# Chunked attention feeding a routed mixture of experts: K block-diagonal over two heads, the zero fill moved, first up products moved, last routing batch reordered

## The chip, the cores and the metric

One core of a Trainium2 chip runs the whole program. The metric is device time in microseconds. The kernel before was run three times: 359.65, 360.88 and 364.33 us, median 360.88. One more execution was profiled; all rows of the trace in this document come from such profiled executions.

The engines that matter: PE (TensorE, matrix products and transposes; PEld is its weight load), DVE (VectorE), ACT (ScalarE), POOL (GpSimd, which here mostly issues DMAs) and SP (SyncE, which only issues DMAs). Every engine works through its own instructions in order and waits on semaphores for the others.

## The reference

Two stages. First, attention in chunks of 32 queries; each chunk sees 16 keys to the left, its own 32, 8 to the right (a window of 56) and 8 memory keys, so 64 scores per query:

```python
batch, n_heads, seq, head_dim = (4, 8, 768, 64)
for c in range(seq // 32):
    k_full = concat([mem_k, k[l_start:r_end]])
    a = softmax(scale * q_c @ k_full.T)
    out[c] = a @ v_full
```

The result, as 3072 tokens of 512 numbers, is `x` of the second stage, a mixture of 8 experts where each token goes to its best two:

```python
noisy_logits = x @ w_gate + log1p(exp(x @ w_noise)) * noise
top2 = the two largest of 8;  top2_w = softmax over them
for e in range(8): out[mask] += top2_w * (relu(x[mask] @ w1[e]) @ w2[e])   # 512 -> 1024 -> 512
```

## The kernel before

**Attention loop (lines 739 to 790).** A pair is two heads of one batch; there are 16 pairs (`NPAIR`), four per batch. The loop is pipelined over `i` = 0 to 16. In iteration `i` the engines get, in this order: the transposes of the softmax of pair i-1 (`PT_pe`, L296) and their copy (`PT_copy`, ACT, L301), maximum and subtraction for pair i (`max_dve`, L282 and L284), transposes and copy of Q of pair i+2 (`turn_pe`, L248 and L249), the value products of pair i-1 (`PV_pe`, L308 and L311), the exponential (`exp_act`, ACT, L289), gate logits of pair i-3 (`logits_pe`, L341), K of pair i+2 (`turn_pe`), the normalisation (`mult_dve`, L322 and L323), transposes of x for pair i-2 (`xT_pe`, L331, copy L333), and the scores of pair i+1 (`scores_pe`).

In `scores_pe` each head occupies 64 partitions, so each head has its own products: 12 with the memory keys (L261), 48 with the windows (L271), and 4 small ones that write -1e30 at the two ends of the sequence (L274): 64 matmuls per pair, each with a weight load. All other products and transposes of a pair are 72 matmuls.

**Loads.** q, k and v are loaded by POOL, six pairs ahead for q and k (`NQ`), and v into four buffers (`NV`). The weights of the first two experts follow in iterations 11 to 14 (`load_w1`, `load_w2`, 1 MB each as stored). The output must be zero before rows are added to it: SP writes 1 MB of zeros in each of iterations 9 to 14 (`zero_fill`, L568).

**Routing (`route`, L348 on).** After each batch of 768 tokens its logits become a list of small steps (s1 to s8): noise, rank of every expert (s1b, s2, s2b), gates (s2c, then s4, which also writes the batch's rows with `nc.sync.dma_start` to the scratch tensor `x_rows`), position of each token within its expert by triangular products (s3, s4b, s5), and a table of token numbers per expert and slot (s5b, s5c on POOL, s6, s7). The steps of batches 0 to 2 are spread over the following iterations (`steps`). `decode` turns a table into row indices, and `gather` has POOL read token rows from `x_rows` by index. Tables of the first batches already hold enough tokens for the first tiles of experts 0 and 1: `begin_first` (in iteration 13) gathers two tiles of 128 tokens for each with `idx_s`, and two further ones for each are gathered behind the loop with `idx_a`; the rest use `idx_f`, after the last batch.

**Experts (`every`, L681).** A generator that yields after each piece of work: `turn` transposes a gathered tile, `up` yields 8 units per half (each 4 matmuls into an `h` bank and a relu), `down` yields per tile of 128 tokens (8 matmuls of 512 columns, a scaling by the gate, and a scatter-add to `out` issued by POOL). `units(k)` runs k pieces. Behind the loop the last batch's routing steps are interleaved with 19 units by hand (L803 to L814); relus and tile copies there go to DVE or ACT by `cnt["by"]`. The order that follows: the four halves of `up` for experts 0 and 1 are 32 units, then `down` for both, then the others.

**Banks.** Transposes rotate through three PSUM banks (`tr`, ring `bankT`); `up` rotates through three (`hring`), which come into being when the loop's own banks are given back (`psE`).

Of the kernel before, what the change touches and what calls it, by code (L numbers as in the profile page):

```python
# [13 lines left out]
BF16 = mybir.dt.bfloat16  # L14
# [10 lines left out]
def kernel(  # L25
# [62 lines left out]
    def body():  # L88
# [107 lines left out]
        neg = const.tile([128, left_ctx], BF16, name="neg")  # L196
        nc.vector.memset(neg, NEG)
        mkT = ap_.tile([128, HP, B * n_mem], BF16, name="mkT", bufs=1)
# [37 lines left out]
        nc.scalar.copy(mkT, p_m)  # L236
# [5 lines left out]
        def turn_pe(n, x):  # L242
            nm, src = ("qT", "kT")[x], qks[n][x]
            dst = ap_.tile([128, 128, SJ], BF16, name=nm, bufs=3)
            p_t = bf16v(tr(), SJ, 128)
            for j in range(SJ):
                for hh in range(2):
                    nc.tensor.transpose(out=p_t[64 * hh:64 * hh + 64, j, :], in_=src[:, hh, j * D:(j + 1) * D], identity=identb)  # L248
            nc.scalar.copy(dst, p_t.rearrange("d j p -> d p j"))  # L249
            st[n][nm] = dst.rearrange("d p j -> d (p j)")  # L250
# [3 lines left out]
        def scores_pe(n):  # L254
            b, hp = divmod(n, HP)
            qT, kT = st[n]["qT"], st[n]["kT"]
            ps = bankS
            for u in range(BT):
                for hh in range(2):
                    hs = slice(64 * hh, 64 * hh + 64)  # L260
                    nc.tensor.matmul(out=ps[:, hh, u * CTX + WIN:(u + 1) * CTX], lhsT=qT[hs, 128 * u:128 * (u + 1)],  # L261
                                     rhs=mkT[hs, hp, b * n_mem:(b + 1) * n_mem], start=True, stop=True)
            for c in range(ncnk):
                u, r = divmod(c, 4)
                for hh in range(2):
                    hs = slice(64 * hh, 64 * hh + 64)
                    lo = left_ctx if c == 0 else 0
                    hi = WIN - right_ctx if c == ncnk - 1 else WIN
                    k0 = chunk * c - left_ctx
                    o = ps[32 * r:32 * r + 32, hh, u * CTX:u * CTX + WIN]  # L270
                    nc.tensor.matmul(out=o[:, lo:hi], lhsT=qT[hs, chunk * c:chunk * (c + 1)], rhs=kT[hs, k0 + lo:k0 + hi], start=True, stop=True)  # L271
                    for a, z in ((0, lo), (hi, WIN)):
                        if z > a:
                            nc.tensor.matmul(out=o[:, a:z], lhsT=onesb[hs, :chunk], rhs=neg[hs, :z - a], start=True, stop=True)  # L274
            st[n]["ps"] = ps[:, :, :BT * CTX].rearrange("p h (u c) -> p h u c", c=CTX)

        def bc4(ap, n):
            return ap.rearrange("p h (u o) -> p h u o", o=1).to_broadcast([128, 2, BT, n])

        def max_dve(n):  # L280
# [3 lines left out]
            nc.vector.tensor_tensor(out=sd, in0=st[n]["ps"], in1=bc4(mx, CTX), op=Alu.subtract)  # L284
            st[n]["sd"] = sd

        def exp_act(n):
            P = ap_.tile([128, BT, 2, CTX], BF16, name="P")
            nc.scalar.activation(out=P.rearrange("p u h c -> p h u c"), in_=st[n]["sd"], func=Act.Exp, scale=scale)  # L289
# [58 lines left out]
        def route(b):  # L348
# [38 lines left out]
            def s2c():  # L387
# [3 lines left out]
                gd = T("gd", [128, BT, E])  # L391
                nc.vector.tensor_tensor(out=gd, in0=nl, in1=bc(m1, E), op=Alu.subtract)
                R["ge"] = T("ge", [128, BT, E])
                nc.scalar.activation(out=R["ge"], in_=gd, func=Act.Exp)
# [13 lines left out]
            def s4():  # L408
# [5 lines left out]
                if b < B - 1:  # L414
                    nc.sync.dma_start(out=xd_part[b][b * S:(b + 1) * S].rearrange("(t p) r -> p t r", p=128), in_=xrows[b])
# [66 lines left out]

            if b == B - 3:
                return (s1,), (s1b, s2), (s2b, s2c), (s3, s4, s4b, spare_a), (s5, s5c, spare_b), (s5b, spare_c), (s6, s7, s8, spare_d, begin_first)
# [465 lines left out]
```

## Time and profile before

| what | value |
|---|---|
| three runs | 359.65, 360.88, 364.33 us |
| the profiled execution, time | 361.64 us |
| its span in the trace | 359.9 us |
| busy in the span: PE / PEld / DVE / ACT / POOL | 289.8 / 182.2 / 162.0 / 134.8 / 230.5 us |
| first maximum (L282) of pair 0 | at 12.67 us |
| last value products (L311) end the loop | at 121.2 us |
| the chain that ended last | the last scatter-add, L666, issued at 351.41 us |

How to read the rows. A row of the timeline gives the start in us, the duration, engine, line, operation, what it writes and reads, how many instructions were merged, and in brackets how long the engine had been idle before and what released it; "issue" means that the trace shows nothing that the engine was waiting for. A row of the waits view gives who waited for whom, the sum in us, how many times, and the longest. A row of the windows view gives a stretch, its length, then busy us and instruction counts for PE, PEld, DVE, ACT and POOL, the granted PE clock (1.00 is full), the mean share of the DMA engines, and GB/s.

### The profile page before, as it was taken

Reading aid. Unit: us, or ns where it says so; the run is one execution under the profiler, and the core shown is the slowest. Engines: PE = TensorE matmul, PEld = TensorE weight load, DVE = VectorE, ACT = ScalarE, POOL = GpSimd, SP = SyncE. Lnnn points to the kernel's source line nnn. Section 1 sums busy time; section 2 is a strip of 40 time slices with the busy share of each in tenths; the row PEclk is TensorE's granted clock in tenths of the full one; section 3 lists DMA queues with packets and bytes.
Section 4 is the critical chain, followed back from the end, with each engine's and each line's share of the span. In section 5 each row is a group of like instructions: output and inputs, shape, how many; then the busy total and the mean of one; then the engine's idle time right before and its main releaser. Section 6 shows DMA issues by size and latency. Waiting matters only on the chain. (4 is left out here: it accounts for less than half of the span.)

```text
span 359.9 us, 8635 instructions
## 1 busy us (share of the span) xinstructions
PE 289.8 (81%) x3583; PEld 182.2 (51%) x3597; DVE 162.0 (45%) x363; ACT 134.8 (37%) x273; POOL 230.5 (64%) x219
## 2 busy tenths in 40 slices
PE   0877788767756767799789999769999999999960
PEld 0755566655535556654555555425555555545420
DVE  7354538966858864432233343123333253323310
ACT  1656456665434326331333332303232432213210
POOL 8987737634533343567888878787887843748181
PEclk9997559985585578999999999969999999999995
DMA  9999999999999955249999999999999997959295
GB/s 106 159 162 185 169 134 122 259 310 150 282 300 233 230 109 124 62 67 169 248 166 194 171 239 164 247 173 190 217 177 189 199 124 115 131 70 131 38 121 74
DMA packets 99162, 60.36 MB, mean 168 GB/s; under 512 B 63536, under 2 KB 84016, under 8 KB 99120
## 3 DMA queue, kind: packets, MB, share of 16 engines
q0 software_dynamic: 82208, 49.84, 101.0%
q1 hardware_dynamic: 16624, 9.86, 9.7%
q8 instruction: 30, 0.49, 0.5%
q14 instruction: 12, 0.10, 0.1%
q10 hardware_dynamic: 288, 0.07, 0.1%
HBM read 65.07 MB, written 23.27 MB: 245 GB/s over the span
## 5 line engine op out<-in xcount | busy, mean ns | idle before, releaser
L638 PEld LDWEIGHTS <-w1t 128*128 128x128 bf16 x576 | 57.3, 101 | 54.5 <-issue 14.1
L666 POOL DMA_INDIRECT out_dram<-ys,idx_f x40 | 62.7, 1569 | 33.3 <-issue 16.0
L654 PE MATMUL bankE<-w2t,htf 128*128 128x512 bf16 x278 | 65.7, 379 | 0.5
L594 POOL DMA_INDIRECT xl<-x_rows,idx_f x48 | 50.0, 1041 | 21.7 <-issue 11.6
L638 PE MATMUL bankE<-xTf,w1t 128*128 128x416 bf16 x256 | 52.8, 349 | 5.7 <-DVE xTf L615 5.4
L665 DVE TENSOR_SCALAR ys<-bankE,gt 128x512 f32<-128x512 f32 (+1 forms) x32 | 21.9, 684 | 68.3 <-PE bankE L654 36.4
L133 POOL DMA_DIRECT2D vp<-in_v_dram x34 | 33.3, 986 | 21.7 <-PE bankO L311 10.8
L663 ACT ACTIVATE ys<-bankE,gt 128x512 f32<-128x512 f32 x24 | 16.5, 688 | 69.5 <-PE bankE L654 49.8
L654 PEld LDWEIGHTS <-htf 128*128 128x128 bf16 x288 | 27.3, 98 | 28.7
L623 DVE TENSOR_SCALAR htf<-bankE 128x416 bf16<-128x416 f32 x32 | 18.9, 591 | 27.5 <-PE bankE L638 25.9
L621 ACT ACTIVATE htf<-bankE 128x416 bf16<-128x416 f32 x32 | 16.6, 517 | 35.2 <-PE bankE L638 34.3
L638 PE MATMUL bankT<-xTf,w1t 128*128 128x416 bf16 x128 | 28.5, 346 | 0.3 <-DVE htf L623 0.3
L638 PE MATMUL bankE<-xTs,w1t 128*128 128x256 bf16 (+1 forms) x128 | 20.7, 302 | 3.9 <-ACT xTs L613 1.8
L282 DVE TENSOR_REDUCE mx<-bankS 128x12 f32<-128x768 f32 x16 | 15.3, 954 | 16.2 <-PE bankS L274 16.2
L654 PE MATMUL bankE<-w2t,hts 128*128 128x512 bf16 x92 | 21.5, 379 | 0.2
L611 PE MATMUL bankT<-identb,xl 128*128 128x128 bf16 (+1 forms) x224 | 19.8, 218 | 2.1 <-DVE xTf L615 1.5
L611 PEld LDWEIGHTS <-xl 128*128 128x128 bf16 (+1 forms) x224 | 15.4, 99 | 11.8 <-issue 4.4
L449 POOL TENSOR_TENSOR col<-mm_all,tl 128x672 f16<-128x672 f16 x4 | 8.0, 2012 | 18.6 <-DVE tl L436 18.6
L308 PE MATMUL bankO<-memv,PT 128*128 128x132 bf16 x96 | 12.0, 282 | 8.5 <-ACT PT L301 5.8
L301 ACT COPY PT<-bankT 128x768 bf16<-128x768 bf16 x16 | 12.8, 798 | 15.9 <-PE bankT L296 14.8
L249 ACT COPY kT<-bankT 128x768 bf16<-128x768 bf16 x16 | 12.7, 797 | 13.6 <-PE bankT L248 12.1
L284 DVE TENSOR_TENSOR sd<-bankS,mx 128x768 f32<-128x768 f32 x16 | 15.3, 958 | 1.4
(180 smaller groups left out, 469.1 us busy)
## 6 DMA issues: line engine op xcount, KB each, us to landing
w1t<-in_moe_w_dram POOLq DMA_DIRECT2D x8, 1024.0 KB
w2t<-in_moe_w_dram POOLq DMA_DIRECT2D x8, 1024.0 KB
out_dram<-zt SPq DMA_DIRECT2D x6, 1024.0 KB, 14.4
vp<-in_v_dram POOLq DMA_DIRECT2D x30, 168.0 KB
x_rows<-xrow SPq DMA_DIRECT2D x4, 792.0 KB, 8.7
qg<-in_q_dram POOLq DMA_DIRECT2D x16, 192.0 KB
kg<-in_k_dram POOLq DMA_DIRECT2D x16, 192.0 KB
xl<-x_rows,idx_f POOLq DMA_INDIRECT x48
```

The source lines that it names most:

```text
L133: nc.gpsimd.dma_start(out=vp[p0 + j:p0 + j + nj, c:c + m, hh, :], in_=bass.AP(v.tensor, v.offset + (hd * S + c * chunk + j - left_ctx) * D ...
L282: nc.vector.tensor_reduce(out=mx, in_=st[n]["ps"], axis=AX, op=Alu.max)
L284: nc.vector.tensor_tensor(out=sd, in0=st[n]["ps"], in1=bc4(mx, CTX), op=Alu.subtract)
L594: nc.gpsimd.indirect_dma_start(out=xl, out_offset=None, in_=xd, in_offset=bass.IndirectOffsetOnAxis(ap=idx[:, c:c + 1], axis=0), bounds_ch ...
L611: nc.tensor.transpose(out=p_t[:, kp, :w], in_=xl[:w, kp * 64:(kp + 1) * 64].bitcast(BF16), identity=identb[:w, :w])
L621: nc.scalar.activation(out=dst, in_=src, func=Act.Relu)
L623: nc.vector.tensor_scalar(out=dst, in0=src, scalar1=0.0, scalar2=None, op0=Alu.max)
L638: nc.tensor.matmul(out=h[:, :hi - lo], lhsT=W1[e][:, kp, f * 128:(f + 1) * 128], rhs=xTs[s][:, kp, lo:hi], start=(kp == 0), stop=(kp == KP ...
L654: nc.tensor.matmul(out=y, lhsT=ht[:, f, o:o + w], rhs=W2[e][:, f, :], start=(f == 0), stop=(f == FB - 1))
L663: nc.scalar.activation(out=ys[:, :wide], in_=y[:, :wide], func=Act.Copy, scale=gate)
L665: nc.vector.tensor_scalar(out=ys[:, :wide], in0=y[:, :wide], scalar1=gate, scalar2=None, op0=Alu.mult)
L666: ins = nc.gpsimd.indirect_dma_start(out=rows, out_offset=bass.IndirectOffsetOnAxis(ap=idx, axis=0), in_=ys[:, :wide], in_offset=None, bou ...
```

## The change

Five things change together.

1. **Scores.** K of a pair is stored block-diagonally, head 0 in partitions 0 to 63 of the first half, head 1 in partitions 64 to 127 of the second, zeros elsewhere, in two buffers zeroed once (`kbufs`); the memory keys likewise (`mkT`). One matmul over 128 partitions then gives both heads: 6 + 24 + 2 = 32 per pair in place of 64. The copy of K from PSUM becomes two copies, one per head, of 64 partitions each. The scores lie in another order, so that the exponential writes one run.
2. **Zero fill.** Issued behind the loop, in three writes of 2 MB, still by SP.
3. **Weights.** `load_w1(0)` in iteration 10, `load_w1(1)` in 12, `load_w2(0)` in 14, `load_w2(1)` behind the loop after the gathers with `idx_a`.
4. **First up products.** Eight units (the first half of expert 0) run in iterations 15 and 16, with `h` in the `tr` ring and relus on ACT. Expert 1's first two tiles are transposed between the last x transposes and the last logits.
5. **Last batch.** Ranks and positions (s2b, s3, s2c, s4b, s5, s5c) come in one group, then the gates' exponential (`s2d`), then s4 with s5b; the batch's rows are written by a DMA that ACT issues. 16 units are interleaved behind the loop in place of 19, so that 24 have been issued before `decode`, with the 8 of the loop.

```diff
-        mkT = ap_.tile([128, HP, B * n_mem], BF16, name="mkT", bufs=1)
+        mkT = ap_.tile([128, HP, B, 2, n_mem], BF16, name="mkT", bufs=1)
+        nc.vector.memset(mkT, 0.0)
+        kbufs = [ap_.tile([128, 2, S], BF16, name=f"kT{i}", bufs=1) for i in range(2)]
+        for kb in kbufs:
+            for hh in range(2):
+                nc.vector.memset(kb[64 * (1 - hh):64 * (1 - hh) + 64, hh, :], 0.0)
...
-            nc.scalar.copy(dst, p_t.rearrange("d j p -> d p j"))
+            if x == 0:
+                dst = ap_.tile([128, 128, SJ], BF16, name="qT", bufs=2)
+                nc.scalar.copy(dst, p_t)
+            else:
+                for hh in range(2):
+                    hs = slice(64 * hh, 64 * hh + 64)
+                    nc.scalar.copy(kbufs[n % 2][hs, hh].rearrange("d (p j) -> d p j", j=SJ), p_t[hs])
...
             for u in range(BT):
-                for hh in range(2):
-                    hs = slice(64 * hh, 64 * hh + 64)
-                    nc.tensor.matmul(out=ps[:, hh, u * CTX + WIN:(u + 1) * CTX], lhsT=qT[hs, 128 * u:128 * (u + 1)],
-                                     rhs=mkT[hs, hp, b * n_mem:(b + 1) * n_mem], start=True, stop=True)
+                nc.tensor.matmul(out=ps[:, u // UB, u % UB, :, WIN:], lhsT=qT[:, 128 * u:128 * (u + 1)], rhs=mkT[:, hp, b], start=True, stop=True)
             for c in range(ncnk):
-                for hh in range(2):
-                    nc.tensor.matmul(out=o[:, lo:hi], lhsT=qT[hs, chunk * c:chunk * (c + 1)], rhs=kT[hs, k0 + lo:k0 + hi], start=True, stop=True)
+                nc.tensor.matmul(out=o[:, :, lo:hi], lhsT=qT[:, chunk * c:chunk * (c + 1)], rhs=kT[:, :, k0 + lo:k0 + hi], start=True, stop=True)
...
-                if b < B - 1:
-                    nc.sync.dma_start(out=xd_part[b][b * S:(b + 1) * S].rearrange("(t p) r -> p t r", p=128), in_=xrows[b])
+                (nc.sync if b < B - 1 else nc.scalar).dma_start(out=xd_part[b][b * S:(b + 1) * S].rearrange("(t p) r -> p t r", p=128), in_=xrows[b])
...
+            if b == B - 1:
+                return (s1,), (s1b, s2), (s2b, s3, s2c, s4b, s5, s5c), (s2d,), (s4, s5b), (s6, s7)
...
-                    h = hring[cnt["h"] % 3]
+                    h = hring[cnt["h"] % 3] if hring else tr()
...
-            if NPAIR - 7 <= i < NPAIR - 1:
-                zero_fill(4 * (i - NPAIR + 7), 4)
-            if i == NPAIR - 5:
+            if i == NPAIR - 6:
                 load_w1(0)
             if i == NPAIR - 4:
-                load_w2(0)
-            if i == NPAIR - 3:
                 load_w1(1)
             if i == NPAIR - 2:
-                load_w2(1)
+                load_w2(0)
             steps(1 if i < NPAIR - 2 else 2)
+            if i >= NPAIR - 1:
+                units(FB // 2)
...
         for s in range(EARLY):
             gather(s, range(FIRST, SEALED), idx_a)
+        for x in range(3):
+            zero_fill(8 * x, 8)
+        load_w2(1)
         logits_pe(NPAIR - 2)
         xT_pe(NPAIR - 1)
-        units(2)
+        cnt["by"] = "dve"
+        for j in range(FIRST):
+            turn(1, j)
         logits_pe(NPAIR - 1)
-        begin, s12, s2, s34, s5, s5b, s678 = route(B - 1)
+        begin, *rest = route(B - 1)
         begin[0]()
         units(3)
         cnt["by"] = "act"
-        for g, more in ((s12, 2), (s2, 3), (s34, 2), (s5, 3), (s5b, 3), (s678, 1)):
+        for g, more in zip(rest, (3, 4, 1, 4, 1)):
             for fn in g:
                 fn()
-            if g is s34:
-                nc.sync.dma_start(out=last, in_=xrows[B - 1])
             units(more)
```

More of the change, by code (lines that the diff above doesn't have):

```diff
@@ L235, in body @@
             nc.tensor.transpose(out=p_m[:, hp, :], in_=mk_nat[:, 2 * hp:2 * hp + 2, :].rearrange("p h d -> p (h d)"), identity=ident)
-        nc.scalar.copy(mkT, p_m)
+        for hh in range(2):
+            nc.scalar.copy(mkT[64 * hh:64 * hh + 64, :, :, hh, :], p_m[64 * hh:64 * hh + 64].rearrange("p h (b m) -> p h b m", m=n_mem))
         st = [dict() for _ in range(NPAIR)]
@@ L263, in scores_pe @@
             for c in range(ncnk):
                 u, r = divmod(c, 4)
-                for hh in range(2):
[L266 to L274, printed above, removed]
@@ L280, in max_dve @@
+                for a, z in ((0, lo), (hi, WIN)):
+                    if z > a:
+                        nc.tensor.matmul(out=o[:, :, a:z], lhsT=onesb[:, :chunk], rhs=neg[:, :, :z - a], start=True, stop=True)
+            st[n]["ps"] = bankS[:, :, :UB * 2 * CTX].rearrange("p x (u c) -> p x u c", c=CTX)
         def max_dve(n):
@@ L685, in part @@
                 for j in range(lo // CAP, (lo + half) // CAP):
-                    turn(s, j)
+                    if s not in gts or (s, j) in got:
+                        turn(s, j)
                 yield from up(s, lo, lo + half)
```

42 lines of the change are left out of this document (23 added, 19 removed).

## The prediction, made before the changed kernel was run

> **What bounds the kernel now.** I read the page first, then the windows view over the stages, then PE's timeline through the attention loop, then the waits.
>
> ```profile
> PE 289.8 (81%) x3583; PEld 182.2 (51%) x3597; DVE 162.0 (45%) x363; ACT 134.8 (37%) x273; POOL 230.5 (64%) x219
> ```
>
> ```profile
> 24.34:107.23 82.89, 61.25 (x1664) 46.58 (x1658) 54.05 (x117) 46.89 (x66) 46.76 (x56) 0.73 1.60 210
> 107.23:121.45 14.22, 9.61 (x208) 7.41 (x206) 12.37 (x29) 6.13 (x10) 4.28 (x4) 0.50 1.30 227
> 121.45:146.65 25.20, 18.20 (x172) 14.53 (x170) 14.38 (x54) 10.24 (x28) 8.12 (x7) 0.76 0.58 128
> 180.00:348.00 168.00, 159.39 (x1019) 85.74 (x1029) 57.83 (x113) 51.68 (x129) 119.69 (x93) 0.98 0.98 161
> ```
>
> ```profile
> 24.34 0.95 DVE L282 TENSOR_REDUCE mx<-bankS 128x12 f32<-128x768 f32 x1
> ...
> 107.23 0.96 DVE L282 TENSOR_REDUCE mx<-bankS 128x12 f32<-128x768 f32 x1 [3.75 <-PE bankS L274]
> ```
>
> From 180 to 348 us PE is busy 159 of 168 us at nearly full clock: the experts are bound by PE, none of their work is taken away, and whatever is won ahead of them moves them earlier. What can be won lies ahead: from the maximum of pair 2 at 24.34 us to that of pair 14 at 107.23 (twelve pairs, 6.9 us each, PE at 0.73 of its clock and idle a quarter of the time), the last pairs, and 25 us behind the loop in which PE, granted 0.76, is idle 7 us while the last batch is routed.
>
> Why is PE idle in the loop? The waits view of 24 to 107 us puts this to "issue":
>
> ```profile
> PE bankS L271 <- issue: 3.7, 8, 0.7
> PE bankT L248 <- issue: 3.0, 2, 1.8
> PE bankO L308 <- ACT PT L301: 2.9, 9, 0.5
> PE bankO L308 <- issue: 2.6, 2, 2.2
> PE bankL L341 <- issue: 2.3, 1, 2.3
> PE bankS L261 <- issue: 2.2, 2, 1.3
> PE bankT L296 <- issue: 1.8, 1, 1.8
> ...
> ```
>
> The issue rows sum to 15.6 us, 1.3 per pair, and no other wait comes near. The timeline between two of these stalls:
>
> ```profile
> 38.59 0.53 PE L248 MATMUL bankT<-identb,qg 128*64 128x128 bf16 x6 [1.28 <-issue]
> 39.06 0.84 PE L308 MATMUL bankO<-memv,PT 128*128 128x132 bf16 x6
> 39.83 0.83 PE L311 MATMUL bankO<-vp,PT 128*32 128x128 bf16 x24
> 40.59 0.33 PE L341 MATMUL bankL<-wgn,xt 128*128 128x16 bf16 x6
> 40.85 0.85 PE L248 MATMUL bankT<-identb,kg 128*64 128x128 bf16 x12
> 41.63 0.82 PE L331 MATMUL bankT<-identb,xrow 128*128 128x128 bf16 x6
> 42.39 0.32 PE L261 MATMUL bankS<-mkT,qT 64*128 64x8 bf16 x12
> 42.64 0.26 PE L271 MATMUL bankS<-kT,qT 64*32 64x40 bf16 x8
> 42.69 0.18 PE L274 MATMUL bankS<-neg,onesb 64*32 64x16 bf16 x2
> 42.70 0.55 PE L271 MATMUL bankS<-kT,qT 64*32 64x56 bf16 x40
> 43.06 0.20 PE L274 MATMUL bankS<-neg,onesb 64*32 64x8 bf16 x2
> 43.19 0.60 PE L296 MATMUL bankT<-identb,P 128*128 128x128 bf16 x4
> 45.62 0.40 PE L296 MATMUL bankT<-identb,P 128*128 128x128 bf16 x2 [1.82 <-issue]
> ```
>
> ```profile
> q8 instruction: 30, 0.49, 0.5%
> ```
>
> From one stall to the next are 6+6+24+6+12+6+12+8+2+40+2+4 = 128 matmuls, each with its weight load: 256 instructions. The instruction queue moved 30 packets for 0.49 MB, about 16 KB each; PE's 3583 + 3597 instructions, in blocks of 256, are 28. So I read the stalls as PE waiting for its next block of instructions while data transfers fill the DMA engines (share 1.60). The block here lasted 45.62 - 38.59 = 7.0 us, of which 1.8 was the stall.
>
> [...]
>
> **Part 1, the scores.** A pair goes from 136 matmuls to 104. Twelve pairs are 384 fewer, three blocks of 128, and each remaining block covers 1.23 pairs instead of 0.94, so there is more work under each fetch. Without stalls an average pair takes 6.9 - 1.3 = 5.6 us; a block then holds 1.23 x 5.6 = 6.9 us of work against the 7.0 us block above. So most stall time should go: I take 12 of 15.6 us; the ends are 15.6 (all) and 15.6 x 32/136 = 3.7 (stalls as long as now, only fewer).
>
> PE time of the scores themselves: now 43.19 - 42.39 = 0.80 us. Afterwards, 24 products of 112 columns, priced by the 24 of 128 columns of L311 on the same 32-wide columns (40.59 - 39.83 = 0.76 us): 0.67; and 6 with the memory keys, by L341 (40.85 - 40.59): 0.26. That is 0.93, or +0.13 per pair, under 2 us for twelve. The gain is in the count, not in PE time.
>
> [...]
>
> ACT gets a second K copy per pair:
>
> ```profile
> 62.01 0.78 ACT L249 COPY kT<-bankT 128x768 bf16<-128x768 bf16 x1
> ```
>
> Half the partitions but the same 768 elements each, so I take the same 0.78 us for each; if the time went by partitions instead, two would cost what one does. ACT is busy 46.9 of 82.9 us in the twelve pairs; 9 us more do not make it the bound as a sum. On the path it delays the softmax transposes' copy, for which PE already waits 0.3 us in nine pairs: I put somewhat under half, 0.35 us a pair or 4 us in twelve, on the path; the ends are 0 and 9. Clock: the granted 0.73 should rise where the stalls go. I add -2 to the sum and make the rest a rival. With one answer: K's two buffers and Q's two instead of three are free in time, since the scores of pair i stand an iteration ahead of the copies for pair i+2; the exponential's new order has as many elements.
>
> Zeroing of the two K buffers and `mkT`:
>
> ```profile
> L165 DVE MEMSET vp<- 128x1536 uint32 x3 | 4.0, 1338 | 0.9 <-issue 0.9
> ...
> 19.37 0.85 PE L248 MATMUL bankT<-identb,qg 128*64 128x128 bf16 x12 [2.07 <-DMA qg<-in_q_dram]
> ```
>
> Four fills of a quarter of that element count are 1.3 us by proportion, 5.4 if each costs a full one. PE waits 2.07 us for q at 19.37 us, so I take nothing; the ends are 0 and 3. Sum for twelve pairs: -12 + 2 + 4 = -6 us, from -20 to +5. Taking 6 MB of zeros out of the loop frees DMA engines under the fetches that remain: I add -3 of the 3.6 us of stalls left over (0 to -3.6).
>
> **Parts 4 and 5, the last pairs and the last batch.**
>
> ```profile
> 129.29 0.21 ACT L356 ACTIVATE ns<-bankL 128x48 f32<-128x48 f32 x1 [3.27 <-PE bankL L341]
> 135.98 0.60 PE L638 MATMUL bankT<-xTs,w1t 128*128 128x256 bf16 x4 [3.23 <-ACT gt L616]
> 139.30 2.67 POOL L449 TENSOR_TENSOR col<-mm_all,tl 128x672 f16<-128x672 f16 x1 [3.94 <-DVE tl L436]
> ...
> 143.37 0.60 PE L638 MATMUL bankT<-xTs,w1t 128*128 128x256 bf16 x4
> ```
>
> Routing starts at 129.29 us, 8 us into the window that begins at 121.45, behind the last value products, because expert 0's transposes, copies and first two units stand between; then it takes 17.4 us to 146.65, where the gathers with `idx_f` begin. The position products (L399) stand in PE's order behind the units that start at 135.98, for which PE has waited 3.23 us, until expert 1's tile copies were done. The change removes both: expert 0's eight units go into pairs 15 and 16, and the position products no longer stand behind a tile copied on ACT. I take 3 us from the first 8, 3.2 for the wait, and 1 for the table step on POOL starting earlier relative to the gates: -7 (-3 to -11). Against it, eight units of at most 0.6 us and 8 transposes enter the last two pairs, where PE is busy 9.6 of 14.2 us: about 5 us of work in 4.6 us of holes, not all usable: +3 (0 to +5). Units ahead of `decode` rise from 19 to 24, so five leave the PE-bound stretch behind it: 5 x 0.6 = -3 (0 to -3).
>
> **Parts 2 and 3, zero fill and weights.**
>
> ```profile
> out_dram<-zt SPq DMA_DIRECT2D x6, 1024.0 KB, 14.4
> 118.07 0.37 SPq L415 DMA_DIRECT2D x_rows<-xrow  x1
> 156.80 1.64 POOL L666 DMA_INDIRECT out_dram<-ys,idx_a  x1 [2.49 <-DVE ys L665]
> SPq L813 <- DMA xl<-x_rows,idx_a: 1.3, 1, 1.3
> ```
>
> SP can start the zeros right behind its write of batch 2's rows (118.07 us now). Three megabytes at a time landed in about 14 us, so six need some 28: to 146 us, ahead of the first scatter-add at 156.80. That is the cover, some 10 us, and the rest shrinks it: the loop's gain moves both ends, the shorter routing only the scatter. If the zeros end late, POOL waits in order, and gathers and weight loads queue behind it. The last rows' write is now issued by ACT; on SP it waited 1.3 us for the `idx_a` gathers, which cost nothing there, but on ACT the relus behind it wait, and PE for them. The gathers and this write now share the engines with the zeros. SP's later read of the gates queues behind the zeros too; the expert stage that follows is 168 us long, so nothing waits for it. I take +2 (0 to +12).
>
> **Sum.** -6 -3 -7 +3 -3 +2 = -14 us, and -2 for the clock: -16. The profiled execution took 361.64 us for a span of 359.9, and the median of the runs is 0.8 below it: 360.9 - 16 = 345 us.
>
> **Rivals.**
> - *The stalls stay.* They are not instruction blocks, or last as long as the data transfers make them: then 3.7 us go instead of 12, the copies and products cost 6, and only the parts behind the loop pay: 345 + 8 + 2 = 355 us. For it: the waits view counts 16 stalls where 12 x 136 / 128 = 13 boundaries lie, and 8 of them stand before L271. Against: the count of 128 between two of the longest. Chance 0.12. [...]
> - *Scores slow down.* Both heads' products take turns where they ran together, 0.8 us a pair more, 13 us in 16, with half hidden under ACT: 345 + 6 = 351 us. Against: L311's 32 ns each. Chance 0.10. [...]
> - *The zeros starve the tail.* Slower. If the zeros share the DMA engines so that the `idx_a` gathers and ACT's row write land 15 us late, ACT holds the relus, PE stops, and the first scatter-add waits too; it decides once the zeros end after the gathers with `idx_f` are due. At half the measured rate six megabytes take 56 us, to 174: 17 past 156.80. With the loop's gain at its poor end (+5 in place of -9) and -7 behind it: 361 + 5 - 7 + 17 = 376; with a third of that delay 365. Against: the DMA share falls to 0.58 at 121 to 147 us. Chance 0.08.
> - *More clock.* Without stalls PE keeps full clock: the 61.3 us of PE work in the twelve pairs, granted 0.73, shrink by up to 0.27 x 61.3 = 17 us; with 10 of them on the path, 335 us. Chance 0.20.
>
> My forecast has 0.50. The forecast's own range is 338 to 352. **Range** 333 to 357: it takes in the clock case and the staying stalls. What a measurement of this kernel can tell from no change is about 2%, 7 us, so faster means under 353.7. Faster: 0.50 + 0.20 + 0.08 of the scores case = 0.78; same: 0.12 + 0.02 + 0.01 = 0.15; slower: 0.07.
>
> **What would show it.** The "issue" rows of PE in the loop fall from 15.6 to under 5 us, 128 matmuls apart where they remain, and a pair takes under 6.2 us. The scores take about 0.93 us at half clock. The K copies show twice per pair at 0.8 us. L356 of the last batch comes within 6 us of the last L311, and the first gather with `idx_f` within 14 us of L356. The zeros end before the first L666. It would be wrong if the issue rows stay, if ACT's row write stands idle for microseconds before it issues, or if the first L666 waits for the zeros.

## The result, and the profile after

| | before | after |
|---|---|---|
| median, range | 360.26 us, 359.23 to 364.33 (4 runs) | 349.19 us, 348.22 to 351.4 (4 runs) |
| profiled execution, span | 361.64, 359.9 us | 351.4, 349.3 us |

The ratio is 0.968, with a 95% interval from 0.959 to 0.977: faster, by 11 us where 16 were predicted. A second series on another chip gave 0.975 (0.971 to 0.979). Ratios here leave out runs over 1.5% above the fastest of their kernel, so they are not always the quotient of two medians, and the profiled executions of e3, e7, e10, e11 and e12 were of that slower kind.

The windows view of the changed kernel, over the twelve pairs from the maximum of pair 2 to that of pair 14 (stretch, its length, busy time of PE, PEld, DVE, ACT and POOL with their counts, granted PE clock, DMA share, GB/s):

```profile
24.72:94.25 69.53, 51.88 (x1280) 42.01 (x1281) 53.46 (x117) 55.37 (x77) 44.52 (x54) 0.85 1.80 176
```

They took 82.89 us before, so 13.4 went here, more than the 10.6 by which the whole span shrank. PE's waits in that stretch:

```profile
PE bankO L313 <- ACT PT L306: 5.5, 8, 1.0
PE bankT L483 <- DVE seen L477: 2.1, 1, 2.1
PE bankT L301 <- ACT kT L263: 2.1, 2, 1.4
PE bankO L316 <- issue: 1.2, 1, 1.2
...
PE bankT L336 <- issue: 1.0, 1, 1.0
...
```

Issue rows sum to 3.3 us now, from 15.6. At the top stand waits for ACT. ACT's timeline over one such pair (start, duration, what was read and written):

```profile
32.38 1.60 ACT L263 COPY kT<-bankT 64x768 bf16<-64x768 bf16 x2 [0.32 <-PE bankT L253]
34.00 0.80 ACT L338 COPY xt<-bankT 128x768 bf16<-128x768 bf16 x1
34.70 0.81 ACT L306 COPY PT<-bankT 128x768 bf16<-128x768 bf16 x1
35.39 0.82 ACT L257 COPY qT<-bankT 128x768 bf16<-128x768 bf16 x1
36.08 0.87 ACT L294 ACTIVATE P<-sd 128x768 bf16<-128x768 f32 x1
37.26 1.60 ACT L263 COPY kT<-bankT 64x768 bf16<-64x768 bf16 x2 [0.32 <-PE bankT L253]
```

From K copy to K copy are 4.88 us, and ACT stands idle for 0.32 of them: where neither a stall nor the routing's steps come in between, ACT is the fullest engine. Whether it sets the pair is tested in e4. The two K copies cost 0.8 us each: half the partitions took no less time than 128.

The loop's time also depends on the granted clock. PE's timeline at one of the stalls that remain, and the windows view around it in steps of 3.41 us:

```profile
43.33 0.61 PE L336 MATMUL bankT<-identb,xrow 128*128 128x128 bf16 x4 [1.00 <-issue]
```

```profile
35.86:39.27 3.41, 3.15 (x102) 2.68 (x99) 2.15 (x3) 3.05 (x5) 2.90 (x4) 1.00 2.40 153
39.27:42.68 3.41, 2.05 (x57) 1.39 (x51) 2.14 (x3) 3.09 (x5) 1.99 (x2) 1.00 2.06 166
42.68:46.10 3.42, 2.77 (x54) 2.44 (x54) 0.96 (x2) 2.33 (x4) 1.71 (x3) 0.50 1.87 169
46.10:49.51 3.41, 3.24 (x57) 2.45 (x54) 2.26 (x4) 2.69 (x6) 3.16 (x4) 0.50 2.19 167
49.51:52.92 3.41, 2.41 (x72) 1.94 (x73) 3.18 (x6) 3.37 (x5) 2.75 (x4) 1.00 2.21 163
```

The granted clock (third number from the end) falls from 1.00 to 0.50 at 42.68 us and comes back at 49.51. The stall ran from 42.33 to 43.33, so the fall came 0.35 us into it, and other idle times of 1.00 us (before 35.56 and 40.44 us) and 1.41 us (before 56.63) left the clock at 1.00: one stall does not decide it. PE was busy for 2.05 of the 3.41 us ahead of the fall. In the trace of this kernel, and in that of the one before, all changes of the clock lie whole multiples of 3.41 us apart. Cut into stretches of that length, the two traces show between 24 and 109 us: the clock fell after stretches in which PE was busy for 0.34 to 0.61 of the time and stayed full after 0.62 to 0.92; once halved, it stayed so after 0.39 to 0.90 and came back after 0.94 or more. From there to 130 us the same shares went with other outcomes: in this kernel the clock stayed full after 0.55 and 0.49 (stretches from 110.95, 121.19 and 124.60 us), and in the kernel before it came back after 0.83 (from 126.58 us). So the shares are readings of two loops, and no experiment set them alone. A stall counts in them with every other wait of PE in its stretch. In the kernel before, with three stalls between 32 and 46 us, the clock was 0.50 in all seven windows of 3 us from 33 to 54 us, the first and the last of which are:

```profile
33.00:36.00 3.00, 3.00 (x108) 2.40 (x100) 1.19 (x2) 1.41 (x2) 2.00 (x4) 0.50 1.80 177
...
51.00:54.00 3.00, 2.43 (x43) 1.84 (x29) 1.92 (x2) 1.58 (x3) 1.31 (x2) 0.50 1.88 128
```

Behind the loop, from the timelines of ACT and POOL:

```profile
118.45 0.21 ACT L361 ACTIVATE ns<-bankL 128x48 f32<-128x48 f32 x1 [0.61 <-PE bankT L620]
...
129.32 0.41 ACTq L421 DMA_DIRECT2D x_rows<-xrow  x1
```

```profile
137.55 1.13 POOL L603 DMA_INDIRECT xl<-x_rows,idx_f  x1 [10.78 <-DVE hts L632]
...
144.24 1.01 POOL L603 DMA_INDIRECT xl<-x_rows,idx_f  x1 [0.30 <-issue]
145.56 1.63 POOL L675 DMA_INDIRECT out_dram<-ys,idx_a  x1 [0.30 <-DVE xTs L624]
```

The last batch's routing starts at 118.45 us (129.29 before). Its rows are written from 129.32 on, and SP's read of the gates, which waits for this write, goes out at 136.96, 7.6 us later. Only then do the gathers with `idx_f` start, although their indices are ready at 133.72. (The releaser named in the gather's row had long been done; the write is what came last.) Then POOL issues six gathers and the first scatter-add without a gap: 8.0 us.

### The profile page after: what moved, and what is told of

It reads as the page before. It is cut to its first block, busy times and chain, and to the rows that moved or that the text cites. A ratio compares the mean times of both kernels' runs of the same rounds, so it can differ in the third digit from the quotient of the medians.

```text
span 349.3 us, 7639 instructions
## 1 busy us (share of the span) xinstructions
PE 277.5 (79%) x3071; PEld 175.5 (50%) x3085; DVE 161.4 (46%) x363; ACT 149.1 (43%) x295; POOL 228.9 (66%) x219
## 5 line engine op out<-in xcount | busy, mean ns | idle before, releaser
L647 PE MATMUL bankE<-xTf,w1t 128*128 128x416 bf16 x256 | 52.0, 346 | 5.4 <-DVE xTf L624 5.4
L263 ACT COPY kT<-bankT 64x768 bf16<-64x768 bf16 x32 | 25.3, 791 | 6.2 <-PE bankT L253 5.8
L647 PE MATMUL bankT<-xTs,w1t 128*128 128x256 bf16 (+1 forms) x88 | 15.2, 314 | 5.8 <-ACT hts L630 4.2
L647 PE MATMUL bankE<-xTs,w1t 128*128 128x256 bf16 (+1 forms) x104 | 16.0, 297 | 2.6 <-DVE xTs L624 1.3
L313 PE MATMUL bankO<-memv,PT 128*128 128x132 bf16 x96 | 9.9, 251 | 9.8 <-ACT PT L306 9.6
L455 POOL TENSOR_TENSOR col<-mm_all,tl 128x672 f16<-128x672 f16 x4 | 6.7, 1670 | 14.4 <-DVE tl L442 14.4
```

The source lines that it names most:

```text
L263: nc.scalar.copy(kbufs[n % 2][hs, hh].rearrange("d (p j) -> d p j", j=SJ), p_t[hs])
L647: nc.tensor.matmul(out=h[:, :hi - lo], lhsT=W1[e][:, kp, f * 128:(f + 1) * 128], rhs=xTs[s][:, kp, lo:hi], start=(kp == 0), stop=(kp == KP ...
```

## The experiments

Twelve kernels ran, on four chips; a time is given as the ratio to the kernel before on the same chip. The readings from which the verdicts come, one profiled execution each: the twelve pairs and what PE does in them (busy time, granted clock, issue rows, waits for ACT's copies PT, kT and xt),

| kernel | twelve pairs | PE busy | clock | issue | ACT copies |
|---|---|---|---|---|---|
| before | 82.9 | 61.3 | 0.73 | 15.6 | 4.0 |
| after | 69.5 | 51.9 | 0.85 | 3.3 | 9.6 |
| after, again (e9) | 69.1 | 50.9 | 0.88 | 1.7 | 9.5 |
| scores only (e1) | 74.1 | 51.2 | 0.85 | 3.5 | 9.3 |
| all but scores (e2) | 77.2 | 57.3 | 0.85 | 15.6 | 2.8 |
| 32 more matmuls (e3) | 80.6 | 61.7 | 0.73 | 10.6 | 5.8 |
| one K copy (e4) | 67.2 | 50.9 | 0.87 | 6.0 | 3.1 |
| zeros in the loop (e7) | 71.0 | 53.6 | 0.81 | 3.8 | 8.9 |

and the way from the loop to the end (us from the span's start; the write is that of the last batch's rows):

| kernel | last value product ends | routing starts | write issued | first `idx_f` gather | first scatter-add | end |
|---|---|---|---|---|---|---|
| before | 121.3 | 129.3 | 137.3 | 146.7 | 156.8 | 359.9 |
| after | 112.7 | 118.5 | 129.3 | 137.6 | 145.6 | 349.3 |
| after, again (e9) | 112.3 | 118.0 | 129.0 | 136.8 | 144.9 | 345.9 |
| e1 | 113.1 | 121.1 | 135.6 | 140.1 | 148.1 | 352.4 |
| w2 in the loop (e6) | 116.8 | 123.4 | 133.0 | 137.6 | 145.6 | 347.8 |
| e7 | 123.2 | 129.1 | 139.4 | 144.8 | 152.8 | 356.7 |
| units behind (e8) | 109.9 | 122.2 | 132.5 | 138.3 | 146.3 | 348.7 |
| w2 behind the loop (e10) | 112.9 | 118.7 | 136.9 | 141.6 | 149.5 | 351.8 |
| the same, relus on DVE (e11) | 114.9 | 120.6 | 134.6 | 139.6 | 147.5 | 351.9 |
| w2 behind a gather (e12) | 116.4 | 122.2 | 132.8 | 137.5 | 146.4 | 355.3 |

The expectations of e3 to e8 give 65.9 us for the twelve pairs of the changed kernel and 7.9 us for its waits on PT. Both were misread; 28.12 us, where the count of the pairs began, is the maximum of pair 3. Twelve pairs take 69.5 us, with 5.5 us of such waits.

**e1: the scores alone**, in the kernel before:

```diff
+        kbufs = [ap_.tile([128, 2, S], BF16, name=f"kT{i}", bufs=1) for i in range(2)]
...
-                    nc.tensor.matmul(out=o[:, lo:hi], lhsT=qT[hs, chunk * c:chunk * (c + 1)], rhs=kT[hs, k0 + lo:k0 + hi], start=True, stop=True)
+                nc.tensor.matmul(out=o[:, :, lo:hi], lhsT=qT[:, chunk * c:chunk * (c + 1)], rhs=kT[:, :, k0 + lo:k0 + hi], start=True, stop=True)
```

> The kernel before with the block-diagonal scores alone; zero fill, weights and the last batch's order stay as before. Theory A (PE waits for its next 256 instructions, so the number of PE instructions sets the loop): PE's issue rows between the maxima of pair 2 and pair 14 fall from 15.6 us to 4 to 6 although the zeros are still in the loop, these twelve pairs take 66 to 70 us instead of 82.9, and the run is 11 to 14 us faster than before, 347 to 350 us. Rival B (the stalls are made by the 6 MB of zeros that share the DMA engines with the fetches): the issue rows stay above 11 us, twelve pairs take over 77 us, the run is less than 5 us faster. Rival C (the gain of the whole change lies in the last batch): twelve pairs shorter by up to 17 us, but the end moves less than 5 us.

Ratio 0.985 (0.977 to 0.993). Theory A is right about the stalls: issue rows fall to 3.5 us though the zeros are still in the loop, so rival B is out. It is wrong about the time: the twelve pairs take 74.1 us, and the gain is some 5 us, not 11. What holds them, in PE's waits:

```profile
PE bankO L313 <- ACT PT L306: 5.6, 8, 1.0
PE bankO L316 <- DMA vp<-in_v_dram: 3.4, 2, 2.6
```

The values arrive late in a loop that runs faster while zeros and weights are moved beside it. What is due to the zeros and what to the weights is not separated here; e7, with the zeros alone put back, has no such wait in these pairs and 1.4 us of it behind them.

**e2: everything but the scores**, the changed kernel with the scores and the single K copy of before.

> The changed kernel with the scores and the single K copy of before; all other parts of the change stay. Theory A (number of PE instructions): issue rows of the twelve pairs at 12 to 16 us, twelve pairs take 78 to 83 us, the run is within 4 us of the kernel before (356 to 361 us). Rival B (zeros in the loop made the stalls): issue rows under 6 us, twelve pairs under 72 us, a run of about 350 us. Rival C (the last batch carries the gain): the loop as before, the run still 8 us or more faster.

Ratio 0.990 (0.984 to 0.995). The issue rows are at 15.6 us, exactly as before, with no zeros in the loop. So the prediction's -3 us, zeros making room for the fetches that remain, is refuted as a mechanism. Rival C is out too: some 4 us are won, not 8. The twelve pairs took 77.2 us, a little under theory A's 78, at a clock of 0.85 beside the same stalls; this execution had the highest mean clock of e2's ten (0.92, the others 0.86 to 0.91).

**e3: the number of matmuls restored**, with work that nobody reads:

```diff
+            for x in range(32):
+                r = x % 4
+                nc.tensor.matmul(out=bankS[32 * r:32 * r + 32, x // 16, 400:408], lhsT=onesb[:, :chunk], rhs=onesb[:, :8], start=True, stop=True)
```

> The changed kernel with 32 more matmuls per pair, of 8 columns each into columns of bankS that nobody reads, so that a pair has 136 matmuls again as before; output unchanged. By the 40 products of 56 columns that took 0.55 us before (14 ns each), 32 cost at most 0.45 us a pair. Theory A (number of PE instructions): the issue rows of the twelve pairs rise from some 4 to 10 to 16 us, twelve pairs take 74 to 83 us instead of 65.9, and the run is 8 to 16 us slower than the changed kernel. Rival D (the arithmetic or the shape of the new scores shortens the loop, not their number): issue rows stay under 6 us, twelve pairs lengthen by at most 5.4 us (12 x 0.45), the run by at most 6.

Ratio 1.000 (0.995 to 1.006): the whole gain is gone. The twelve pairs take 80.6 us, 11.0 more than in the changed kernel. Issue rows are back to 10.6. Between two of the longest stalls stands, in PE's timeline:

```profile
80.57 0.28 PE L272 MATMUL bankS<-mkT,qT 128*128 128x16 bf16 x5 [1.74 <-issue]
80.78 0.24 PE L279 MATMUL bankS<-kT,qT 128*32 128x80 bf16 x4
80.82 0.19 PE L282 MATMUL bankS<-neg,onesb 128*32 128x32 bf16 x1
80.85 0.41 PE L279 MATMUL bankS<-kT,qT 128*32 128x112 bf16 x20
81.10 0.17 PE L282 MATMUL bankS<-neg,onesb 128*32 128x16 bf16 x1
81.10 0.41 PE L285 MATMUL bankS<-onesb 128*32 128x8 bf16 x32
81.44 0.51 PE L304 MATMUL bankT<-identb,P 128*128 128x128 bf16 x6
81.87 0.53 PE L253 MATMUL bankT<-identb,qg 128*64 128x128 bf16 x12
82.84 0.52 PE L316 MATMUL bankO<-memv,PT 128*128 128x132 bf16 x6 [0.44 <-ACT PT L309]
83.28 0.52 PE L319 MATMUL bankO<-vp,PT 128*32 128x128 bf16 x24
83.74 0.31 PE L349 MATMUL bankL<-wgn,xt 128*128 128x16 bf16 x6
83.97 0.52 PE L253 MATMUL bankT<-identb,kg 128*64 128x128 bf16 x11
87.86 0.31 PE L253 MATMUL bankT<-identb,kg 128*64 128x128 bf16 x1 [3.36 <-issue]
```

The sum is 5+4+1+20+1+32+6+12+6+24+6+11 = 128 matmuls, with their weight loads 256 instructions. The stall does not fall on a step of the algorithm: it cuts the twelve K transposes after the eleventh. The fillers themselves took 0.41 us here, by estimate some 5 us in twelve pairs; the other 6 of the 11.0 come with the stalls and a clock that is back at 0.73. Rival D allowed 5.4 us in all, and is out.

**e4: without the second K copy**, to price it:

```diff
-                for hh in range(2):
+                for hh in range(1):
```

> The changed kernel without the copy of head 1's K (its rows in the K buffers stay zero), so the scores of every second head with the sequence's own keys are left out of the computation and its output is not the reference's. It prices the second copy. Theory E (ACT sets the loop of the changed kernel): PE's wait for the softmax transposes' copy falls from 7.9 us to 2 to 4 in the twelve pairs, these take 57 to 61 us instead of 65.9 (0.4 to 0.7 us of the copy's 0.79 a pair come back), and the run is 6 to 11 us faster than the changed kernel. Rival F (the clock or the stalls that remain set the loop, and the copy is hidden): twelve pairs within 2 us of 65.9, the run within 2 us.

Ratio 0.969 (0.963 to 0.976), as the changed kernel. PE's waits for PT fall to 2.9 us as theory E said, but the twelve pairs shrink by 2.3 us only, to 67.2: issue rows return from 3.3 to 6.0, and 2.2 us go to late Q loads (0.7 in the changed kernel). So ACT's second copy does not set the pair: most of what its removal frees is waited for elsewhere. Counted from 69.5 us, rival F is nearer: the copy is mostly hidden.

**e5: the second K copy on DVE:**

```diff
-                    nc.scalar.copy(kbufs[n % 2][hs, hh]...
+                    (nc.vector.tensor_copy if hh else nc.scalar.copy)(kbufs[n % 2][hs, hh]...
```

> The changed kernel with head 1's K copy on DVE instead of ACT; nothing is left out. Theory E (ACT sets the loop): ACT loses 0.79 us a pair; DVE, busy 54 of 82.9 us before, takes one more copy a pair. The pair shortens by 0.2 to 0.6 us, PE's wait for the softmax transposes' copy falls below 5 us of 7.9, the run is 3 to 8 us faster than the changed kernel. Rival F (copy hidden, or DVE becomes the bound in ACT's place): twelve pairs within 2 us of 65.9 or longer, the run within 2 us of the changed kernel or slower.

Ratio 1.025 (1.019 to 1.031), slower than before the change; twelve pairs 87.0 us. The waits view of DVE shows why:

```profile
DVE kT L263 <- ACT kT L263: 16.9, 11, 2.0
```

The two halves are written one after the other, so DVE stands and waits for ACT's half, and everything queued behind the copy on DVE waits with it; then PE waits 12.6 us for that copy. The run does not say what two copies side by side would cost.

**e6 to e8: three moves behind and in the loop.** e6 issues expert 1's second weights in the last pair instead of behind the zeros:

```diff
+            if i == NPAIR - 1:
+                load_w2(1)
...
-        load_w2(1)
```

> The changed kernel with expert 1's second weights issued in the last pair of the loop instead of behind the zeros, so ahead of the gathers with idx_a. Theory G (ACT's write of the last batch's rows lands late, 7.6 us instead of 3.8 before, because it shares the DMA engines with that 12 us load): the write lands in 4 to 5 us, the gathers with idx_f start 2 to 4 us earlier than 137.55 us, and the run is 2 to 4 us faster. Rival H (the write shares with the zeros, or its form is slow on ACT's queue): it still lands 7 us or more after its issue, the run within 1.5 us. Against the edit: POOL's gathers with idx_a stand behind the load's issue, and instruction fetches in the last pairs share with it.

The write lands as theory G said:

```profile
133.02 0.41 ACTq L421 DMA_DIRECT2D x_rows<-xrow  x1
```

```profile
137.06 0.37 SPq L850 DMA_DIRECT2D gov<-x_rows  x1
```

That is 4.0 us, not 7.6, so ACT's queue is not slow (rival H). But the gathers start no earlier, since this execution's loop ended 4 us later: pair 13 took 10.7 us, where the changed kernel needed 7.0. The edit is not shown to be the reason, as the load is issued behind that pair, and e12, whose loop is that of the changed kernel, needed 9.9. Ratio 0.959 (0.951 to 0.967), some 3 us below the first series of the changed kernel and 6 below the second, though not beside either on one chip. It may be the best version of all; that is not settled.

e7 puts the zeros back into the loop, 1 MB in each of six passes:

```diff
+            if NPAIR - 7 <= i < NPAIR - 1:
+                zero_fill(4 * (i - NPAIR + 7), 4)
...
-        for x in range(3):
-            zero_fill(8 * x, 8)
```

> The changed kernel with the zero fill back in six iterations of the loop, 1 MB in each. Theory A with the prediction's term for it (3 us, 0 to 3.6): issue rows of the twelve pairs rise from some 4 to 5 to 8 us, the run is 1 to 4 us slower. Rival B (zeros in the loop made the stalls): issue rows over 10 us, the run 8 us or more slower. Rival J (zeros do nothing in the loop once it has fewer instructions, and behind the loop they delay the tail): the run is the same or up to 3 us faster.

Ratio 0.983 (0.976 to 0.989), some 5 us slower than the first series and 3 than the second, on other chips. The issue rows stay at 3.8 us, below theory A's 5 to 8 and far below rival B's 10, and the twelve pairs cost 1.5 more. The loss lies in the last pairs, where the last value product ends 10.5 us later than in the changed kernel. PE's timeline there:

```profile
115.76 1.04 PE L620 MATMUL bankT<-identb,xl 128*128 128x128 bf16 x8 [8.19 <-DMA xl<-x_rows,idx_s]
```

and POOL's, ahead of it:

```profile
97.47 0.81 POOL L556 DMA_DIRECT2D w1t<-in_moe_w_dram  x1 [6.52 <-DMA vp<-in_v_dram]
98.66 1.16 POOL L603 DMA_INDIRECT xl<-x_rows,idx_s  x1 [0.37 <-DVE rec L327]
103.55 1.04 POOL L603 DMA_INDIRECT xl<-x_rows,idx_s  x1 [3.73 <-DMA w1t<-in_moe_w_dram]
```

Expert 0's work in the last pairs needs rows that are gathered late, since POOL waits in order for late values and weights. So the two edits depend on each other: with the zeros in the loop, PE waits 8.2 us for the units' rows.

e8 leaves the zeros behind, and takes the units out of the last pairs:

```diff
-            if i >= NPAIR - 1:
-                units(FB // 2)
...
+        units(FB)
```

> The changed kernel with expert 0's eight first up products behind the loop, ahead of expert 1's transposes, instead of four in each of the last two passes. Theory K (they fill holes of PE in the last two pairs, but only in part): the last value product ends 3 to 5 us earlier than 112.7 us, routing of the last batch starts within 1.5 us of 118.4 us, and the run is 0 to 3 us slower. Rival L (in the loop they cost their full time, since ACT's relus stand in line with the copies that set the pair): the last value product is 5 us or more earlier, the routing starts 1.5 us or more earlier, the run is 1 to 3 us faster.

Ratio 0.970 (0.964 to 0.976), no difference that can be told. The last value product ends 2.8 us earlier (theory K: 3 to 5), routing starts 3.7 us later, and as the row write then lands in 5.2 us, the first scatter-add comes 0.7 us later. Theory K holds for the time of the run, not for the start of routing.

**e9 to e11: where to put the load**, beside the changed kernel itself. e9 is the changed kernel itself. e10:

```diff
+        load_w2(1)
         decode(tabs[(B - 2) % 2][:, :EARLY * NT], idx_a, None)
...
-        load_w2(1)
```

and e11 besides:

```diff
-        cnt = {"h": 0, "y": 0, "flip": 0, "by": "act"}
+        cnt = {"h": 0, "y": 0, "flip": 0, "by": "dve"}
```

> The changed kernel once more, as the measure for the two that run with it on this chip. By the ratio of its first runs, 0.968 of the kernel before; twelve pairs in 68 to 71 us, the last rows' write 7 to 9 us ahead of the first gather with idx_f, and some 203 us from the first scatter-add to the end, as in every kernel so far (201.5 to 204.3).

> The changed kernel with expert 1's second weights issued directly behind the loop, ahead of the decoding for idx_a, so some 12 us earlier (about 109 instead of 121.6 us) and not in the loop. Theory G (the last rows' write lands late because that load shares the DMA engines with it): the first gather with idx_f stands 4 to 5.5 us behind the write's issue instead of 8.2, the first scatter-add comes 3 to 4 us earlier, and as it is some 203 us from there to the end, the run is 3 to 4 us faster than the changed kernel beside it. Rival H (the write is slow on ACT's queue, or the zeros delay it): 7 us or more as now, the run within 1.5 us. Rival M (PE bounds everything behind decode, so an earlier scatter-add is not an earlier end): the write lands early, and the run is within 1 us.

> As the run before it, and the relus, tile copies and gates of expert 0's first up products in the last two pairs on DVE instead of ACT. Theory N (in the last two pairs ACT is the bound, so that work of expert 0 lengthens the pairs through ACT): the last value product ends 1 to 3 us earlier, the run is 1 to 3 us faster than the run before it. Rival O (DVE is as full there as ACT, or the units cost PE's own time): within 1 us, or slower by up to 2.

Ratios 0.975 (0.971 to 0.979), 0.976 (0.971 to 0.981) and 0.977 (0.972 to 0.982): no difference. In e10 the first gather stands 4.7 us behind the write's issue, so theory G holds once more. But in this execution the write is issued 8 us later than in e9, and PE's timeline shows why:

```profile
131.66 1.19 PE L620 MATMUL bankT<-identb,xl 128*128 128x128 bf16 x8 [7.04 <-DMA xl<-x_rows,idx_a]
```

With weights as well as zeros ahead of them, the gathers with `idx_a` landed in 13.7 us (6.7 in the changed kernel). PE waited for them, ACT for PE, and the write stands behind that work in ACT's order. The span of this execution is 5.9 us longer than e9's, while the ratios do not differ, so a delay of this size is shown for this execution alone. In e11 the last value product ends 2.0 us later than in e10, and PE waits for DVE instead (rival O).

**e12: the load behind the first gather:**

```diff
-            gather(s, sets[s][1], idx_f)
+            gather(s, sets[s][1][:1], idx_f)
+            if s == EARLY:
+                load_w2(1)
+            gather(s, sets[s][1][1:], idx_f)
```

> The changed kernel with expert 1's second weights issued behind the first gather with idx_f instead of ahead of the last batch, some 13 us later (about 135 instead of 121.6 us). Theory G (the last rows' write lands late because that load shares the DMA engines with it): with the zeros done by then, the write lands 3.8 to 5 us behind its issue instead of 7.6, the first gather with idx_f starts 3 us earlier. The load costs POOL 1.0 us among the gathers and lands 8 to 12 us later, at 143 to 147 us, about when the second expert's down products want it (148.7 less 3): the first scatter-add comes 1.5 to 2.5 us earlier, the run is 1 to 3 us faster than the changed kernel. Rival P (the load then shares with the gathers and PE waits for it): the write lands early all the same, the gathers land 6 us or more behind their issue instead of 2.9, the run is the same or up to 4 us slower. Rival H (the write is slow on ACT's queue whatever runs beside it): it lands 7 us or more behind its issue.

Ratio 0.982 (0.975 to 0.988): above both series of the changed kernel, though the intervals overlap and the chips differ. That fits rival P (the same or up to 4 us slower), and theory G's gain did not come. The write lands in 4.0 us, with the load out of the way:

```profile
132.84 0.41 ACTq L421 DMA_DIRECT2D x_rows<-xrow  x1
```

```profile
136.88 0.37 SPq L851 DMA_DIRECT2D gov<-x_rows  x1
```

and PE waits for the gathers that are now issued around it:

```profile
PE bankT L620 <- DMA xl<-x_rows,idx_f: 6.3, 1, 6.3
```

Theory G is shown for the write itself. In e6, e10, e11 and e12, where the load is elsewhere, the write lands in 4.0 to 4.1 us. Beside the load it takes 4.8 us in e7, 5.2 in e8, 7.2 in e9 and 7.6 in the changed kernel; in the last two the load, issued at 121.11 and 121.56 us, lands 12.9 and 13.0 us later, 5.0 and 5.2 us behind the write's issue. In the trace of the changed kernel 208 packets of the load begin between the first and the last of the write's 784. The zeros' last packet there had ended at 126.2 us, 3.2 us before the write was issued, so the zeros do not delay it. An earlier write is not yet an earlier end: in e10 and e12 something else then came late (rows for PE by 7.0 and 6.3 us), with the zeros, two weights, two sets of gathers and the write all issued between the loop's last pairs and the first scatter-add.

## Why the prediction was right, and where its sizes were off

The direction, the main mechanism and the range held; the forecast was 4 us too low. Term by term, from the two profiled executions (10.6 us of span; the terms are rounded):

| step | predicted | measured |
|---|---|---|
| up to pair 2, and twelve pairs (-6 -3 -2) | -11 | -13.0 |
| units in the last pairs | +3 | +4.4 |
| last batch: start of routing, routing | -7 | -4.4 |
| contention at the row write | +2 | +3.8 |
| first gather to end (five units fewer) | -3 | -1.5 |
| sum | -16 | -10.6 |

**The stalls are blocks of instructions.** Shown: -12 was predicted for part 1 and 12.3 us went; the stalls follow the number of matmuls in e1, e2 and e3, in e3 with nothing else changed. Counted from the first matmul of the program, all 50 stalls of 0.6 us or more in the loops of the 14 profiles stand at the same places, multiples of 128 apart to within one recorded matmul: behind 606 recorded matmuls, for instance, in the kernel before (38.59 us), after (43.33 us) and in five variants, be it in Q's transposes or in those of x. In the DMA view, the microsecond from 36.00 to 37.00 of the kernel before holds one packet of instructions:

```profile
q8 instruction: 1, 0.02, 6.1%
```

It landed at 36.98 us; PE's stall began at 37.31 and ended at 38.59. Of the eleven such stalls in the traces of the kernels before and after, ten ended 1.3 to 1.6 us behind the landing of such a packet of 16 KB, one 2.1. In e5, where 128 matmuls last longest (by estimate some 8.9 us: 87.0 / 12 us a pair, 104 matmuls each), none is left. The 16 stalls that the prediction counted against 13 block ends contain many short waits; the eight of 0.6 us or more all stand on block ends. The rival "the stalls stay" is out.

**The twelve pairs came out near the forecast for other reasons than its sum.** PE's busy time fell by 9.4 us and its waits by 4.0. How much of the first is the clock, put at -2, stays open. By the mean clock, 61.25 us at 0.73 and 51.88 at 0.85 are almost the same work (44.7 and 44.1 us at full clock); but e2, with the matmuls of before, was busy for 57.3 us at 0.85, by which the clock gave 4.0 us and the fewer matmuls 5.4. Either way the sum, which put PE's busy time at +2 - 2, had too little; that the total came out near is luck in part. The rival "more clock" had the mechanism, but not the end: of the 12.3 us of stalls, 8.3 came back as other waits, 5.6 of them behind ACT's copies (4.0 before, 9.6 after), the rest behind DVE's routing steps and Q loads. The +4 for the second copy was of the right order as a wait; e4 shows that only 2.3 us would be won by removing it. The ends that the prediction gave for the twelve pairs, -20 to +5, do not follow from its terms: these add up to -14 (all stalls go, the scores cost 2, the rest nothing) and +10 (-3.7 + 2 + 9 + 3).

**The scores** cost less than the +2: at full clock they took 0.74 us before (27.49 to 28.23 us) and 0.64 after (27.34 to 27.98 us), at half clock 0.80 (42.39 to 43.19 us) and 0.97 (43.73 to 44.70 us), as predicted (0.93). The 0.8 us a pair of the rival "scores slow down" is shown by no run: they became 0.10 us shorter at full clock and 0.17 longer at half. That rival is out.

**The zeros** have nothing to do with the stalls (e2, e7), so the -3 rested on a wrong mechanism. Putting them back cost 1.5 us in the twelve pairs and more in the last pairs, through late values and late gathers (e7). They did not starve the tail either: their last packet ended at 126.2 us, 19 us ahead of the first scatter-add.

**The last batch was over-sized.** "L356 of the last batch comes within 6 us of the last L311" held (5.7), "the first gather with `idx_f` within 14 us of L356" did not: 19.1. Routing itself shrank by 2.1 us, not 4.2, and 3.8 us were lost between the indices and the gathers. The prediction named this contention, as "the gathers and this write now share the engines with the zeros"; the partner was the load of weights behind them, as the zeros had ended.

**The five units** were taken to leave a stretch that PE bounds. In the first 35 us from the first gather with `idx_f` on, PE of the changed kernel is busy for 28.3, and POOL issues one DMA after the other with mostly 0.3 us between them; only later is PE near full. That POOL sets the pace there is read off the trace, not tested. From the first scatter-add to the end are 203.1 us before and 203.7 after, 201 to 204.4 in all variants except e12, whose weights came late. Before, the first scatter-add waited 2.49 us for its products; that wait went, and no more.

## What to carry to other kernels

Where an engine shows idle time without a releaser, count its instructions between two stalls: if the count is the same whatever work lies there (here 128 matmuls, or a multiple), instructions are what must be saved. Price a removed stall by what is late next, not by its length: here two thirds of the stalls (8.3 of 12.3 us) came back as waits on ACT, DVE and loads, and most of the gain came as less busy time of PE (61.3 to 51.9 us), with fewer matmuls and a higher granted clock (0.73 to 0.85). Look at the granted clock and at PE's busy share around a stall as well; that a stall costs more than its length through the clock was not tested here. Before moving a load out of a crowded stretch, list what each new neighbour would wait for; two of the three places tried here (e10, e12) moved the wait, and for the third (e6) it is not settled.

## What the runs showed of the hardware

All figures are from the traces of the kernels before and after. The changes of the granted clock lay whole multiples of 3.41 us apart; in the loops (24 to 109 us) it fell behind stretches of that length with PE busy for 0.34 to 0.61 of the time, and came back behind stretches with 0.94 or more, while from 109 to 130 us it stayed full behind 0.49 and came back behind 0.83. Of eleven stalls of 0.6 us or more for which PE's releaser is "issue", ten ended 1.3 to 1.6 us behind the landing of a 16 KB packet of the instruction queue, one 2.1. A copy of 64 partitions on ACT took as long as one of 128 (0.79 us, and 0.80 in the kernel before, for 768 elements each). Products over 128 rows of which half are zeros took 0.64 us at full clock where twice as many over 64 rows took 0.74, and 0.97 at half clock where those took 0.80: two heads side by side on 64 rows each were ahead at half clock alone.
